# The last chunk's spectrum rows of the last batch, from SBUF to SBUF: squared-ReLU attention followed by a gated FFT convolution, in one kernel

## The chip, the cores and the metric

The kernel runs on one core of one Trainium2 chip. The metric is the device time of one execution in microseconds. Times of single instructions come from one profiled execution of the kernel before.

## The reference

Eight batches of 3136 rows go through an attention without softmax and then through a gated long convolution. Cut to what matters:

```
def attention(u, v, z):                       # u, v: 8 x 3136 x 256, z: 8 x 3136 x 64
    scores = z @ z.T / S                      # S = 3136
    return u * (relu(scores) ** 2 @ v)

def hyena(x, w_proj, filter_fft, w_out):      # x: the attention's result
    x1, x2, x3 = split(x @ w_proj, 3)
    X2 = rfft(x2, axis=seq)
    H  = rfft(filter_fft, axis=seq)
    return (x1 * irfft(X2 * H, axis=seq) * x3) @ w_out
```

## The kernel before, in words

All matrix operands are bf16, all sums are fp32 in PSUM. The 3136 columns of a batch are cut into seven chunks (512, 512, 512, 512, 512, 256, 320 columns; `CHUNKS`), which hold 25 tiles of 128 columns. For each chunk the kernel computes scores (`ps_s<-zT_t` in the profile), squares their ReLU (`R_t`, `A_t`), weighs v with them (`ps_s<-A_t,v_t`; some blocks are mirrored by DMA transposes, `M_t`, `M2e_t`, `M2o_t`), and multiplies the sum by u, which gives `xT_t`. From `xT_t` two things are made. The gates are `x1 * x3` (`ps_s<-xT_t,wp`, then `x_t`, `gate_t`). The spectrum starts with x2 (in `to_spectrum`: `ps_s<-wp,xT_t`, copied to SBUF as `x2`, which the profile shows as `x_t`).

The FFT of length 3136 is done as 64 x 49. The first stage, `dft1`, is a matmul with the table `T1` over 64 rows (`ps_s<-x_t,T`); its result is copied to the SBUF tile `s_t`, and SyncE's queue writes it to the DRAM scratch `D1` (`put`, L1065 and L1068). Row index and frequency index have to change places between the stages, and this detour through DRAM does it: the second stage reads `D1` with 49 rows on partitions 0 to 48 and another 49 on partitions 64 to 112 (`load_spec`, in the last batch `load_parts`, L1114). Four input tiles hold one quarter of the frequencies each; two are from the pool `l_p` (`spec_in_t`), two from `gs_p` (`gs_t`). The second stage (`forward`, `ps_s<-spec_in_t,S` and `ps_s<-gs_t,S`) has eight groups, two for each input tile. Each group is copied out of PSUM (`xh` or `R_t`), multiplied twice by H on VectorE (L1394), goes through the inverse of 49 (`inverse2`, `ps_s<-xh,TZ`, `ps_s<-R_t,TZ`), is copied out (`M_t`, `M2e_t`, `M2o_t`, `A_t`, `uT_t`), and is written to a second DRAM scratch, `D2` (L1443). When all of it has landed, `add_end` reads D2 chunk by chunk (`load_c`, L1128), runs the inverse of 64 (`ps_s<-T,A_t` in the last batch, `ps_s<-T,conv_in_t` and `ps_s<-T,v_t` in the one before), multiplies by the gate (`yT_t`, `uT_t`, L1499), by `w_out` (`ps_s<-wo,...`), copies the result (`ost_t`, `v_t`, `R_t`, `xh`, `gs_t`) and stores it (`out_dram`, L1548).

All engines run orders that are written out: a table `ORDER` lists the tasks, `ENGINES` says for each copy or elementwise task whether ScalarE or VectorE does it, `BANKS` which of four PSUM pairs a task gets. Each engine's instructions, and each DMA queue (SyncE, ScalarE, GpSimd), run strictly in that order. While TensorE has nothing to do, the table may have it multiply the identity (`ps_s<-ident`), work that is thrown away.

In the last batch nothing of a following batch fills the waits. The work of kind `FZ` does: the gates of the last batch, and the ends of chunks 4 to 6 of the batch before. In the stage before this, `load_parts` reads each input tile in two pieces. Rows 0 to 39, which come from chunks 0 to 4, are read early; rows 40 to 48, from chunks 5 and 6, are read when the last chunk has been written:

```
LATE_Q = 2 * T0[NC - 2]
...
a = on("SP", lambda: go(0, LATE_Q), 1.0, first, [home.slots], ...)
if home is gs_p:
    return a, on("ACT", lambda: go(LATE_Q, N2, nc.scalar), 1.1, [*first, *rest, (a, ISSUED)], ...), box
return a, on("SP", lambda: go(LATE_Q, N2), 1.0, [*first, *rest, (a, ISSUED)], ...), box
```

## Time and profile before

| | |
|---|---|
| time, median of 3 runs | 942.79 us (938.34 to 945.0) |
| the profiled execution | 942.77 us, of which 940.9 us from the first to the last instruction |
| TensorE busy | 914.0 us (97%), granted clock 0.997 |
| VectorE, ScalarE, GpSimd busy | 838.7 us (89%), 819.6 us (87%), 247.6 us (26%) |
| chain that ended last | TensorE 83%, ScalarE 5%, VectorE 5%, DMA 5% |
| DMA | 170.70 MB, mean 181 GB/s |

TensorE is busy almost without a gap until the last batch's last chunk has been weighed, some 55 us before the end. The rest is one dependent chain through both spectrum stages, with left-over work laid beside it.

### The profile page before, as it was taken

How to read it: one execution, taken by the hardware profiler on the slowest of the kernel's cores; microseconds unless marked ns; L12 is line 12 of the kernel's file. 1: busy time of each engine (PE TensorE's matmuls, PEld its weight loads, DVE VectorE, ACT ScalarE, POOL GpSimd, SP SyncE). 2: the span in 40 equal slices, each digit the busy share in tenths (PEclk: the TensorE clock that was granted, in tenths of full speed). 3: DMA queues.
4: the chain of work that ended last, by engine and by line, in shares of the span. 5: the costliest groups of instructions: out<-in, count | busy, mean ns of one | idle time of the engine just before them, and what ended most of it. 6: DMA issues, size and time to landing. Idle time of an engine off the chain costs nothing.

```text
span 940.9 us, 30306 instructions
## 1 busy us (share of the span) xinstructions
PE 914.0 (97%) x12425; PEld 555.4 (59%) x12425; DVE 838.7 (89%) x1117; ACT 819.6 (87%) x952; POOL 247.6 (26%) x585
## 2 busy tenths in 40 slices
PE   8999999999999999999999999999999999999985
PEld 3445655566554666556565565666565666676654
DVE  8886899999888998999889988999988999899795
ACT  7877898999889998898989999899988999899673
POOL 5143322332332312223122231333123141101030
PEclk9999999999999999999999999999999999999999
DMA  9899899989999789998999989998999979898867
GB/s 158 155 176 163 141 156 197 185 144 173 169 218 201 151 190 168 206 200 146 192 173 212 177 160 189 178 223 149 200 167 208 224 128 202 202 205 140 207 193 232
DMA packets 331644, 170.70 MB, mean 181 GB/s; under 512 B 242887, under 2 KB 307143, under 8 KB 331505
## 3 DMA queue, kind: packets, MB, share of 16 engines
q1 hardware_dynamic: 301624, 131.98, 70.2%
q0 software_dynamic: 29168, 35.13, 25.8%
q8 instruction: 97, 1.59, 0.7%
q10 hardware_dynamic: 712, 1.66, 0.6%
q14 instruction: 43, 0.34, 0.2%
HBM read 90.26 MB, written 53.05 MB: 152 GB/s over the span
## 4 chain that ended last, share of the span: by engine, by line
PE 83%; ACT 5%; DMA 5%; DVE 5%; issue 2%; SPq 0%; POOL 0%; DVEq 0%; ACTq 0%; POOLq 0%
PE ps_s L553 82%; DMA M_t<-A_t 3%; ACT R_t L1956 2%; DVE xh L1394 1%; DVE A_t L1967 1%; DMA zn_t<-in_z_dram 1%; ACT A_t L1965 1%; DVE xT_t L2012 1%; DMA A_t<-spec 0%; ACT xh L619 0%; DMA spec<-uT_t 0%; ACT ost_t L619 0%; ACT s_t L619 0%; DVE gs_t L623 0%; ACT R_t L619 0%
## 5 line engine op out<-in xcount | busy, mean ns | idle before, releaser
L553 PE MATMUL ps_s<-A_t,v_t 64*128 64x512 bf16 (+5 forms) x4766 | 515.7, 352 | 1.1 <-DVE A_t L1967 1.0
L553 PEld LDWEIGHTS <-v_t 64*128 64x128 bf16 (+1 forms) x6528 | 305.8, 98 | 185.9 <-PE ps_s L553 19.2
L1956 ACT ACTIVATE R_t<-ps_s 128x1024 f32<-128x1024 f32 (+3 forms) x359 | 336.8, 961 | 50.4 <-PE ps_s L553 47.2
L1965 ACT ACTIVATE A_t<-R_t 128x1024 bf16<-128x1024 f32 (+2 forms) x281 | 271.8, 992 | 12.0 <-DVE R_t L1958 4.9
L1967 DVE SCALAR_TENSOR_TENSOR A_t<-R_t 128x1024 bf16<-128x1024 f32 (+3 forms) x211 | 233.6, 1123 | 17.6 <-ACT R_t L1956 10.3
L553 PE MATMUL ps_s<-zT_t 64*128 64x512 bf16 (+5 forms) x1186 | 191.4, 352 | 4.4 <-DVE gate_t L1293 1.7
L1958 DVE TENSOR_SCALAR R_t<-ps_s 128x1024 f32<-128x1024 f32 (+4 forms) x153 | 170.3, 1124 | 23.7 <-PE ps_s L553 13.3
L676 POOL COPY tick<-A_t 1x1 bf16<-1x1 bf16 x159 | 54.3, 341 | 426.0 <-ACT A_t L1965 262.0
L553 PE MATMUL ps_s<-xT_t,wp 64*128 64x512 bf16 (+3 forms) x976 | 124.3, 352 | 0.5 <-DVE R_t L1958 0.4
L553 PEld LDWEIGHTS <-zT_t 64*128 64x128 bf16 (+1 forms) x1219 | 68.9, 97 | 52.8 <-issue 9.8
L553 PE MATMUL ps_s<-M_t,v_t 64*128 64x512 bf16 (+4 forms) x860 | 96.6, 353 | 1.8 <-DMA M_t<-A_t 1.7
L619 ACT ACTIVATE x_t<-ps_s 128x1024 bf16<-128x1024 f32 (+3 forms) x75 | 69.4, 927 | 20.9 <-PE ps_s L553 18.1
L1394 DVE TENSOR_TENSOR xh<-xh,H 128x1024 bf16<-128x1024 bf16 x120 | 81.8, 685 | 2.9 <-ACT xh L619 2.0
L1293 DVE TENSOR_TENSOR gate_t<-ps_s,x_t 128x512 bf16<-128x512 f32 (+2 forms) x112 | 64.5, 617 | 12.4 <-PE ps_s L553 10.3
L2012 DVE TENSOR_TENSOR xT_t<-ps_s,uT_t 128x512 bf16<-128x512 f32 (+2 forms) x112 | 64.0, 614 | 6.5 <-PE ps_s L553 6.1
L1499 DVE TENSOR_TENSOR yT_t<-ps_s,gate_t 128x1024 bf16<-128x1024 f32 (+2 forms) x53 | 56.9, 1078 | 12.9 <-PE ps_s L553 11.7
L553 PEld LDWEIGHTS <-wp 64*128 64x128 bf16 (+1 forms) x976 | 47.8, 96 | 30.0 <-PE ps_s L553 2.0
L553 PE MATMUL ps_s<-wp,xT_t 64*128 64x256 bf16 (+2 forms) x944 | 64.0, 266 | 0.1
L553 PE MATMUL ps_s<-wo,yT_t 64*128 64x256 bf16 (+2 forms) x904 | 62.3, 266 | 1.0 <-DVE yT_t L1499 0.5
L662 POOL DMA_DIRECT2D un_t<-in_u_dram x112 | 58.1, 519 | 18.5 <-issue 16.0
L688 POOL DMA_DIRECT2D v_t<-in_v_dram x112 | 58.4, 525 | 13.6 <-issue 10.3
L553 PEld LDWEIGHTS <-xT_t 64*128 64x128 bf16 (+1 forms) x944 | 43.5, 97 | 19.1 <-issue 0.6
(157 smaller groups left out, 910.2 us busy)
## 6 DMA issues: line engine op xcount, KB each, us to landing
out_dram<-ost_t SPq DMA_DIRECT2D x60, 256.0 KB
spec_in_t<-spec SPq DMA_DIRECT2D x56, 192.0 KB
spec<-gs_t SPq DMA_DIRECT2D x56, 192.0 KB
v_t<-in_v_dram POOLq DMA_DIRECT2D x80, 128.0 KB, 4.5
un_t<-in_u_dram POOLq DMA_DIRECT2D x80, 128.0 KB, 4.5
spec<-s_t SPq DMA_DIRECT2D x40, 256.0 KB
conv_in_t<-spec SPq DMA_DIRECT2D x34, 256.0 KB
out_dram<-ost_t SPq DMA_DIRECT2D x18, 128.0 KB
```

What stands on the lines that cost most here:

```text
L553: got = nc.tensor.matmul(o, *args, **kw)
L619: got = nc.scalar.activation(out_, in_, AF.Copy)
L662: nc.gpsimd.dma_start(out=t[ds(j * N1, N1), lo - t0 : hi - t0, :], in_=x[:, n2 : n2 + hi - lo, :])
L688: nc.gpsimd.dma_start(out=t[ds(j * N1, N1), ds(v_at(a), (b - a) * D)], in_=r[:, n2 + a - lo : n2 + b - lo, :].rearrange("p t d -> p (t d)"),)
L1293: has_read(nc.vector.tensor_tensor(o[:, :, ::-1] if h == 0 else o, p, x, ALU.mult), p)
L1394: nc.vector.tensor_tensor(x[:, 1 - i], x[:, 0], h, ALU.mult)
L1499: has_read(nc.vector.tensor_tensor(yb["y"][:, :, 0:w], p, gates[b, c][:, :, 0:w], ALU.mult), p)
L1956: has_read(nc.scalar.activation(r, p, AF.Relu), p)
L1958: has_read(nc.vector.tensor_single_scalar(r, p, 0.0, ALU.max), p)
L1965: nc.scalar.activation(a, r, AF.Square, scale=1.0 / float(S))
L1967: nc.vector.scalar_tensor_tensor(a, r, inv_s2, r, ALU.mult, ALU.mult)
L2012: has_read(nc.vector.tensor_tensor(x[:, :, ::-1] if h == 0 else x, f, ut, ALU.mult), f)
```

## The change

In the last batch, the first-stage result of the last chunk (rows 44 to 48 of both halves) is no longer written to D1 and read back. Ten DMAs take it from the SBUF tile `s_t` straight into the four input tiles; each of them gathers 32 pieces of 512 bytes (for row 48, 64 pieces of 256 bytes) from 32 partitions into the whole row of one partition, across all four tiles. SyncE issues four, ScalarE three and GpSimd three. For this the four tiles become one SBUF tensor, `grid`, and the pools `l_p` and `gs_p` become parts of it. Rows 0 to 43 still come from D1, now in one piece for each tile (`load_most`), once chunks 0 to 5 are written; those of the `l_p` parts are issued by SyncE, those of the `gs_p` parts by GpSimd. The copies of this chunk's `x2` and `s_t` out of PSUM are split in two, one for each bank (`by_bank`). `ORDER`, `ENGINES` and `BANKS` are new tables.

```diff
-    gs_p = Pool("gs", 2, [P, 8, D], BF16)
-    l_p = Pool("spec_in", 2, [P, 8, D], BF16)
+    grid = const.tile([P, 4 * 8, D], BF16, name="grid")
+    class Part:
+        def __init__(self, *at):
+            self.at, self.slots, self.n = at, Slots(len(at)), 0
+        def tile(self, shape=None, dtype=None):
+            t = grid[:, ds(8 * self.at[self.n % len(self.at)], 8), :]
...
+    l_p, gs_p = Part(0, 1), Part(2, 3)
...
+    def by_bank(n, ev, a, deps, split):
+        got = []
+        for b in ((0,), (1,)) if split else ((0, 1),):
+            x = slice(b[0], b[-1] + 1)
+            t = job(None, lambda e, x=x: ev(e, x), both(n * len(b)), deps)
+            t.frees.append((a, 0))
+            got.append(t)
+        a.holders = len(got)
+        return got
+
+    def straight(s, t0, nt):
+        m, w = nt // 2, nt * P
+        x = s[:, 0 : 2 * w].rearrange("p (b w) -> p b w", b=2)
+        got = []
+        for q in range(2 * t0, min(2 * (t0 + nt), N2)):
+            t, h = q // 2 - t0, q % 2
+            for r in range(2):
+                at = ds(h * N1 + r * 2 * NJ, 2 * NJ)
+                o = grid[r * N1 + q : r * N1 + q + 1]
+                if t == nt - 1 and nt % 2:
+                    got.append((o.rearrange("p x (b d) -> p x b d", b=2), x[at, :, m * D : w]))
+                else:
+                    got.append((o, x[at, t // m, ds(t % m * D, D)]))
+        return got
...
-        b_ = job(None, ev, both(2 * w), [a2])
+        b_ = by_bank(w, ev, a, [a2], split)
+        if split:
+            def go(e, i):
+                by = {"SP": nc.sync, "ACT": nc.scalar, "POOL": nc.gpsimd}[e]
+                for o, x in straight(s["s"], t0, nt)[i::3]:
+                    by.dma_start(out=o, in_=x)
+            return [(e, lambda e=e, i=i: go(e, i), b_) for i, e in enumerate(("SP", "ACT", "POOL"))]
...
-    LATE_Q = 2 * T0[NC - 2]
+    LATE_Q = 2 * T0[NC - 1]
-    def load_parts(src, j0, nj, first, rest, home):
+    def load_most(src, j0, nj, deps, home, by):
         box = {}
+        def go():
+            box["t"] = home.tile([P, 8, D], BF16)
+            rows = src[0:S, :].rearrange("(q r x) d -> r q x d", r=2, x=2 * NJ)[:, 0:LATE_Q, ds(2 * j0, 2 * nj), :]
+            for r in range(2):
+                {"SP": nc.sync, "POOL": nc.gpsimd}[by].dma_start(out=box["t"][r * N1 : r * N1 + LATE_Q, 0 : 2 * nj, :], in_=rows[r])
+        return on(by, go, 1.0, deps, [home.slots], moves=0.36 * nj, late=0.5), box
...
-            if g % 2 == 0 and final:
-                after_q = [(before[-1], ISSUED)] if before and homes[g // 2] is gs_p else []
-                ldb[0] = load_parts(D1[b % 2], 2 * g, 4, [*puts[:early], *after_q], puts[early:], homes[g // 2])
+            if g == 0 and final:
+                parts_ = []
+                for i, home in enumerate(homes):
+                    after_q = [(before[-1], ISSUED)] if before and home is gs_p else []
+                    after_q += [(parts_[-1][0], ISSUED)] if i % 2 else []
+                    parts_.append(load_most(D1[b % 2], 4 * i, 4, [*puts, *after_q], home, "POOL" if home is gs_p else "SP"))
+                lasts_in = []
+                for e, go, made_ in direct:
+                    lasts_in.append(on(e, go, 1.8, [*made_, *((t, ISSUED) for t, _ in parts_)], prio=-1, moves=0.1, late=0.5))
+            if final:
+                ld, ibox = parts_[g // 2]
+                more = lasts_in
```

Of the tables, one line of `ORDER` near its end before and after reads:

```diff
-    "R]KLKER^KYR=vTR#R}R_PFvUR~KFPGR{vVKGPHPRSLR[SMS0PLR|PMSQPNvWSRvXSNPOSXKMKHSYS1SbKNSSScvYSOKOSPSTS2SU"
```

What the new tables mean is seen in the engines' orders. Over the first 89% of TensorE's rows (22,137 of 24,852), and about as far on the other four engines, the instructions and their order are the same as before, except for which PSUM pair an instruction uses. Behind that point the orders part.

On SyncE's queue, around the second stage's input, `spec_1_60` is D1 and `spec_1_62` is D2 of the last batch, `spec_0_61` is D2 of the batch before. Before:

```order
L1065 DMA spec_1_60<-s_t 128x2x256
L1114 DMA gs_t<-spec_1_60 40x2048 x2
L1114 DMA spec_in_t<-spec_1_60 40x2048 x2
L1114 DMA gs_t<-spec_1_60 40x2048 x2
L1128 DMA v_t<-spec_0_61 128x2x256
L1128 DMA v_t<-spec_0_61 128x3x256
L1128 DMA conv_in_t<-spec_0_61 128x4x256
L1065 DMA spec_1_60<-s_t 128x2x256
L1068 DMA spec_1_60<-s_t 128x1x128
L1128 DMA conv_in_t<-spec_0_61 128x4x256
L1114 DMA spec_in_t<-spec_1_60 9x2048 x4
```

And with the change, at the same place:

```order
L1104 DMA spec_1_60<-s_t 128x2x256
L1170 DMA v_t<-spec_0_61 128x2x256
L1170 DMA conv_in_t<-spec_0_61 128x4x256 x2
L1603 DMA out_dram<-ost_t 64x512 x2
L1159 DMA grid<-spec_1_60 44x2048 x4
L1119 DMA grid<-s_t 1x32x256 x3
L1119 DMA grid<-s_t 1x64x128
```

The first line of both is the write of chunk 5. Before, the large reads stand around it and the write and read of the last chunk (L1065, L1068, `9x2048`) far behind; now the large reads stand behind it, and the four direct transfers follow them at once.

On GpSimd, the end of the program. Before:

```order
L1548 DMA out_dram<-ost_t 64x1024 x4
L1548 DMA out_dram<-v_t 64x1024 x2
L1548 DMA out_dram<-ost_t 64x1024 x2
L1443 DMA spec_1_62<-M_t 48x2048
...
L1548 DMA out_dram<-v_t 64x512 x2
L1548 DMA out_dram<-v_t 64x768
L1548 DMA out_dram<-v_t 64x512
L1548 DMA out_dram<-ost_t 64x1024 x2
L1548 DMA out_dram<-R_t 64x1024
L1548 DMA out_dram<-xh_118 64x1024
```

With the change:

```order
L1159 DMA grid<-spec_1_60 44x2048 x4
L1119 DMA grid<-s_t 1x32x256 x2
L1119 DMA grid<-s_t 1x64x128
...
L1603 DMA out_dram<-ost_t 64x1024 x2
L1603 DMA out_dram<-v_t 64x768
L1603 DMA out_dram<-v_t 64x512
L1603 DMA out_dram<-R_t 64x1024
L1603 DMA out_dram<-xh_118 64x1024
L1603 DMA out_dram<-ost_t 64x1024 x4
L1603 DMA out_dram<-v_t 64x1024 x2
```

`ost_t` and `v_t` are results of the batch before the last, `R_t` and `xh_118` the first of the last batch. Six stores of 256 KB (64 x 1024 fp32 each) of the batch before the last, which stood ahead of the first D2 write or of `R_t`, now stand behind `xh_118`.

On TensorE, just ahead of the second stage (`spec_in_t,S` before, `grid,S` after; the LDWEIGHTS row ahead of each matmul loads its weights). Before:

```order
L553 MATMUL ps_s_142<-T_215,conv_in_t 128x2x64
L553 LDWEIGHTS ident
L553 MATMUL ps_s_140<-ident 128x512
...
L553 LDWEIGHTS S_216
L553 MATMUL ps_s_140<-spec_in_t,S_216 64x256
```

With the change:

```order
L567 MATMUL ps_s_134<-T_210,v_t 128x128
L567 LDWEIGHTS v_t
L567 MATMUL ps_s_134<-T_210,v_t 128x2x64
...
L567 LDWEIGHTS S_211
L567 MATMUL ps_s_137<-grid,S_211 64x256
```

The 26 identity matmuls of the last 50 us are gone altogether. Otherwise TensorE's matmuls are the same in sum, but 16 matmuls of a gate projection (`xT_t,wp`, 512 columns) and 16 of an output projection (`wo,yT_t`, 8 of 256 and 8 of 128 columns) that stood ahead of the last weighing (`A_t,v_t`) now stand behind it.

More of the change, by code (lines that the diff above doesn't have):

```diff
@@ L187 @@
[L187 to L191 removed]
+    "0123012312313213213213212310313013131032032032032320230201201012012023203023020323010210210212313213"
@@ L1051, in view, with ev @@
             return x[:, 0 : 2 * w].rearrange("p (b w) -> p b w", b=2)
-        def ev(e):
-            copy(e, view(s["s"]), box["p"][:, :, 0:w])
+        def ev(e, x=slice(0, 2)):
+            copy(e, view(s["s"])[:, x], box["p"][:, x, 0:w])
         def put():
@@ L1248 @@
             h_done += evs
+    direct = []
     gates, made = {}, {}
@@ L1326, in view, with ev2 @@
                 return x[:, 0 : 2 * w].rearrange("p (b w) -> p b w", b=2)
-            def ev2(e):
-                copy(e, view(box2["x"]), box["p"][:, :, 0:w])
+            def ev2(e, x=slice(0, 2)):
+                copy(e, view(box2["x"])[:, x], box["p"][:, x, 0:w])
             cost = c_pe(*[D] * (2 * m), *([P] * 2 if n % 2 else []))
             a, a2, box = two("FA", mm, cost, xt_tasks, [x2_p.slots])
-            e2 = job(None, ev2, both(2 * w), [a2])
-            e2.frees.append((a, 0))
+            end = b == B - 1 and c == NC - 1
+            e2 = by_bank(w, ev2, a, [a2], end)
             users.append(a2)
@@ L1339, in get @@
                 return x[:, m * D : w] if k is None else x[:, 0 : m * D]
-            puts.append(
-                dft1(
-                    "FA", get, t0, n, D1[b % 2], [e2, t1_done], (a, 1),
-                    late=LATE_PUT,
-                )
-            )
+            got = dft1(
+                "FA", get, t0, n, D1[b % 2], [*e2, t1_done], (a, 1),
+                late=LATE_PUT, split=end,
+            )
+            if end:
+                direct.extend(got)
+            else:
+                puts.append(got)
         if b == B - 1 and c == NC - 1:
@@ L1371, in add_spectrum @@
             per, gh = 2 * len(mine), outs[sets.index(mine)]
-            if g % 2 == 0 and final:
-                after_q = [(before[-1], ISSUED)] if before and homes[g // 2] is gs_p else []
-                ldb[0] = load_parts(D1[b % 2], 2 * g, 4, [*puts[:early], *after_q], puts[early:], homes[g // 2])
+            if g == 0 and final:
[10 more added lines that the diff above has]
+                more = lasts_in
             elif g % 2 == 0:
                 ldb[0] = load_spec(D1[b % 2], 2 * g, 4, puts, LATE_LOAD)
-            ld, *more, ibox = ldb[0]
+            if not final:
+                ld, *more, ibox = ldb[0]
             xb = {}
```

246 lines of the change are left out of this document (120 added, 126 removed).

## The prediction

> **What bounds the kernel now.** I read the page first, then the chain of waits, then the time-ordered rows of each engine from 860 us on, and last a table of stretches.
>
> ```profile
> PE 914.0 (97%) x12425; PEld 555.4 (59%) x12425; DVE 838.7 (89%) x1117; ACT 819.6 (87%) x952; POOL 247.6 (26%) x585
> PE   8999999999999999999999999999999999999985
> ```
>
> TensorE is the bound over the whole program, in every slice but the first and the last two. The orders of all engines are the same for nine tenths of the program, so I expect nothing of the change there. What counts is the tail: how long the chain from the last chunk to the last store takes, and what TensorE has to do beside it.
>
> The tail's first part, from the rows of TensorE, ScalarE and SyncE's queue:
>
> ```profile
> 888.40 0.72 PE L553 MATMUL ps_s<-x_t,T 64*128 64x256 bf16 x6
> 889.16 0.81 ACT L619 ACTIVATE s_t<-ps_s 128x768 bf16<-128x768 f32 x1 [0.83 <-PE ps_s L553]
> 889.99 0.36 SPq L1065 DMA_DIRECT2D spec<-s_t x1
> 890.41 0.58 SPq L1068 DMA_DIRECT2D spec<-s_t x1
> 894.38 1.68 SPq L1114 DMA_DIRECT2D spec_in_t<-spec x4
> 896.70 0.61 PE L553 MATMUL ps_s<-ident 64*128 64x512 bf16 x4
> 897.24 1.15 PE L553 MATMUL ps_s<-spec_in_t,S 49*64 49x256 bf16 x11
> ```
>
> The first stage's result is in SBUF at 889.97. Its write to D1 is issued by 890.99, the read can start only at 894.38, and the second stage starts at 897.24: **7.27 us** of detour. TensorE hides most of it with left-over work, but the identity matmuls show that this work has run out.
>
> The rest of the chain:
>
> ```profile
> 898.21 0.60 ACT L619 ACTIVATE xh<-ps_s 128x512 bf16<-128x512 f32 x1 [0.56 <-PE ps_s L553]
> 911.61 0.85 ACT L619 ACTIVATE uT_t<-ps_s 128x512 bf16<-128x512 f32 x1
> 913.70 3.91 DMA spec<-uT_t
> 914.63 1.24 PE L553 MATMUL ps_s<-ident 64*128 64x512 bf16 x10
> 918.48 1.03 PE L553 MATMUL ps_s<-ident 64*128 64x512 bf16 x8
> 919.02 4.18 DMA A_t<-spec
> 920.72 0.40 PE L553 MATMUL ps_s<-T,A_t 64*128 64x128 bf16 x8 [1.22 <-DMA A_t<-spec]
> 933.49 0.38 PE L553 MATMUL ps_s<-wo,yT_t 64*128 64x256 bf16 x4
> ```
>
> The second stage and its inverse take from 898.21 to 912.46 (911.61 + 0.85), 14.25 us, bound by the copies and multiplications: in the stretches below, ScalarE and VectorE are full from 900 to 908 and TensorE is not. The detour through D2 takes from there to 920.72, 8.26 us; the last stage ends on TensorE at 933.87. Then come the last stores.
>
> ```profile
> 900.00:904.00 4.00, 3.51 (x71) 2.15 (x63) 4.00 (x7) 4.00 (x9) 0.00 (x0) 1.00 0.28 89
> 904.00:908.00 4.00, 2.92 (x58) 1.59 (x56) 4.00 (x8) 4.00 (x10) 2.15 (x4) 1.00 0.62 116
> 920.00:924.00 4.00, 2.66 (x64) 1.95 (x66) 2.36 (x2) 0.60 (x1) 1.03 (x2) 1.00 0.83 243
> 924.00:928.00 4.00, 4.00 (x86) 3.14 (x82) 2.58 (x4) 3.14 (x6) 1.06 (x2) 1.00 0.96 286
> 928.00:932.00 4.00, 3.10 (x64) 2.13 (x58) 3.87 (x7) 1.20 (x3) 0.00 (x0) 1.00 0.96 326
> 938.00:939.00 1.00, 0.00 (x0) 0.00 (x0) 0.00 (x0) 0.00 (x0) 0.00 (x0) 0.67 0.88 308
> 939.00:940.00 1.00, 0.00 (x0) 0.00 (x0) 0.00 (x0) 0.00 (x0) 0.00 (x0) 0.50 0.01 3
> ```
>
> The last two columns are the DMA engines' busy share and GB/s. From 924 on the DMA engines are full, at 286 to 326 GB/s. The last bytes move at 939.0, and the span ends 1.9 us later. From 900 to 908 they are nearly idle.
>
> **The change, step by step.** All against the profiled execution: span 940.9, time 942.77, 1.87 apart; the median of the runs is 942.79, so the same number serves.
>
> *Less TensorE work ahead of the last chunk.* One gate projection (16 matmuls) and 16 output matmuls go behind it:
>
> ```profile
> 880.16 1.02 ACT L619 ACTIVATE x_t<-ps_s 128x1024 bf16<-128x1024 f32 x1 [0.50 <-PE ps_s L553]
> 883.90 1.29 DVE L1293 TENSOR_TENSOR gate_t<-ps_s,x_t 128x512 bf16<-128x512 f32 x2 [1.76 <-PE ps_s L553]
> 882.22 0.59 PE L553 MATMUL ps_s<-xT_t,wp 64*128 64x512 bf16 x4
> 882.65 0.71 PE L553 MATMUL ps_s<-A_t,v_t 64*128 64x320 bf16 x8
> 911.77 0.50 PE L553 MATMUL ps_s<-wo,yT_t 64*128 64x256 bf16 x8
> 912.12 0.59 PE L553 MATMUL ps_s<-xT_t,wp 64*128 64x512 bf16 x4
> ```
>
> Four projection matmuls take 0.43 (882.22 to 882.65), so 16 take 1.72; eight output matmuls of this kind take 0.35 (911.77 to 912.12), so 16 about 0.65. With the projection go its copy (1.02) and its gate product (1.29), so ScalarE and VectorE have less to do there too. Up to the first-stage matmul itself 0.2 goes the other way. First stage at 886.3 instead of 888.40: **-2.1**. If ScalarE or VectorE hold it up, half of this is lost.
>
> *Split copies.* `s_t` is copied in two halves of 384 columns on two engines at once. No copy of 384 from PSUM to bf16 stands in the trace; 512 takes 0.60 (898.21) and 768 takes 0.81, so 0.5, and 0.3 gained (0.2 to 0.4). The same split of `x_t` one step earlier is worth nothing: gate projection lies beside it. `s_t` is ready at 887.5 instead of 889.97, **-2.5 in all**.
>
> *Ten direct transfers for the detour.* SyncE issues four, at 1.68/4 = 0.42 each: 1.7. From issue to data, no row shows a transfer into single partitions. The nearest are a read of D1 of 36 KB (issued by 895.2, used at 897.24: 2.0), a GpSimd load of 64 KB, and the write to D2 above (3.91):
>
> ```profile
> un_t<-in_u_dram POOLq DMA_DIRECT2D x1, 64.0 KB, 2.4
> ```
>
> I take 2.4: it is the nearest in size. 887.5 + 1.7 + 2.4 = **891.6** for the second stage's start instead of 897.24; with 2.0 and 3.9 it is 891.2 and 893.1. One thing gets worse: before, the first group needed two transfers, now it needs rows that all ten bring. Removed are two writes and eight small reads.
>
> The direct rows land in few partitions (44 to 48 and 108 to 112). [...]
>
> *The large reads.* They now wait for chunk 5's write, and nothing is read before:
>
> ```profile
> 880.71 0.69 DVE L623 CAST s_t<-ps_s 128x512 bf16<-128x512 f32 x1 [0.33 <-PE ps_s L553]
> 882.65 0.51 SPq L1065 DMA_DIRECT2D spec<-s_t x1
> 883.20 0.78 SPq L1114 DMA_DIRECT2D gs_t<-spec x2
> 884.00:886.00 2.00, 2.00 (x30) 1.17 (x24) 1.80 (x5) 0.00 (x0) 0.00 (x0) 1.00 1.06 308
> ```
>
> This write went out 1.25 behind its copy, after reads that it now stands ahead of; and the copy itself comes earlier by about the 2.1 above. I expect the write by 880, landed 3.4 later (as 890.99 to 894.38), 1.44 MB (8 x 180 KB) at 308 GB/s in 4.7: there by 888.5, hidden behind the direct rows with 3 us to spare.
>
> *Second stage and inverse.* The same 27 copies of 512 columns and one of 1024 on ScalarE, but one more of 1024 (`x_t`, 1.02) between them: 14.25 + 0.9. It ends at about 907.7 instead of 912.46: **-4.7**.
>
> *The D2 detour* stays at 8.26: first `T,A_t` at 916.0. At the rate above (0.107 for 512 columns) the matmuls that stand between the last inverse and `T,A_t` come to 8.7 us of left-over work, where 5.3 and 18 identity matmuls stood; with the 0.8 between the last inverse matmul and its copy's end it just fits. Cover is used up here; each us that it runs over is a us.
>
> *The last stage and the stores.* By the same rate TensorE has 9.3 us of work there instead of 9.8, so it ends about 928.7, and on the old distance (940.9 - 933.87 = 7.0) the span would end at **935.7**. But GpSimd's queue now holds six stores of 256 KB (1.57 MB) behind the store of `xh`:
>
> ```profile
> 904.42 1.06 POOL L1548 DMA_DIRECT2D out_dram<-ost_t x2 [5.42 <-ACT ost_t L619]
> 923.25 0.40 PE L553 MATMUL ps_s<-T,A_t 64*128 64x128 bf16 x8 [0.61 <-DMA A_t<-spec]
> 925.91 1.08 ACT L619 ACTIVATE xh<-ps_s 128x512 f32<-128x512 f32 x2
> 927.29 0.52 POOL L1548 DMA_DIRECT2D out_dram<-xh  x1 [0.57 <-ACT xh L619]
> ```
>
> Before, stores like that of 904.42 ran when the DMA engines were idle. The copy of `xh` ended 6.3 after the first `T,A_t`. A second pair of copies now lies ahead of it (1.1), and the wait of 0.6 at 923.25 goes, since the chunk that waited is read later: 6.8, so 922.8. Of 3.21 MB of the last batch's output (3136 x 256 x 4 bytes) about 0.65 have moved by then (2.2 us at 0.3). 3.21 + 1.57 - 0.65 = 4.1 MB at 306 GB/s (mean of 286 and 326) take 13.4, from 923.1 to 936.5, and 1.9 more give a span of 938.4; at 326 it is 937.6. The stores end last, not TensorE. I take the middle, 938.0: -2.9, a time of **939.8 us**.
>
> **Rivals.** *The stores are hidden after all* (other transfers leave room, the queues share well): TensorE ends it, span 935.7 and time 937.6; with a direct landing of 2.0 (-0.4), the extra copy hidden (-0.9) and the wait at 923.25 gone from TensorE's end too (-0.6), 935.7. For it: the row at 928 shows 326 GB/s. Against: 286 just before, at the same busy share.
>
> *The direct rows come late.* If writes to single partitions go one after the other, or chunk 5's write is not as early as I think (with 882.65 for it the reads end at about 891.5 and the direct rows queue behind), the second stage starts at 894 to 896. Then `xh` is copied at 925.2 to 927.2 and by the sum above (at 326 GB/s) the time is 942 to 944. This is also the case in which the change does not do what it says.
>
> *Slower: GpSimd's queue.* The six stores behind `xh` add 1.57/0.306 = 5.1 us of transfers to the stretch that the DMA engines already fill. The span gets longer than 940.9 once 0.3 + 13.4 + 1.9 after the copy of `xh` pass it, that is when this copy ends later than 925.3, only 1.7 before its old 926.99. An overrun of 2.5 of the left-over work after the inverse does it, or a start of the second stage at 894.1. Just there, and at the 243 GB/s of the row at 920 (16.9 for 4.1 MB) instead of 306, the span is 944.4 and the time 946.3; at 275, 944.3.
>
> **How the numbers follow.** Forecast 0.5 (own range 938 to 941.8); stores hidden 0.2; direct rows late 0.15; slower by the queue 0.12; the rest, 0.03, outside. The range takes in the first three and the lower half of the fourth, and 1 us below the best of them, since the three times of before differ by 6.7: 934.5 to 945. About 1% (9.4 us) is what a measurement of this kernel can tell from no change. No case reaches 933.4: faster by over 1% gets 0.04. Slower by over 1% (952.2) would need the queue's case with more than I can price: 0.04. Within 1%: 0.92.
>
> **What would show it.** The first `grid,S` matmul should stand near 891.6, 4.1 behind the copy of `s_t`; the first `T,A_t` near 916; no identity matmuls after the start. GB/s near 300 should hold from about 920 to the last byte, with stores of `ost_t` and `v_t` by GpSimd behind `xh`. I am wrong on the sum if TensorE idles for over 1 us between 908 and 916, if the large reads land after the direct rows, or if the last bytes move well before 935 or after 938.

## The result: 7 us slower, where 3 us faster was forecast

| | before | after |
|---|---|---|
| median of 7 runs each (us) | 942.79 | 949.82 |
| lowest to highest | 938.34 to 949.53 | 946.87 to 952.47 |
| ratio, 95% interval | | 1.0079 (1.0050 to 1.0109) |
| profiled execution: time, span | 942.77, 940.9 | 950.02, 948.2 |

The interval excludes 1: the change costs 0.5 to 1.1%. The forecast was 939.8 and the range ended at 945; the ratio itself lies within the 1% that had been given 0.92. The page of the changed kernel shows nearly the same work on each engine; only the last slices differ (TensorE 2 and its clock 6 in the last one, the clock 7 two slices earlier):

```profile
PE 913.4 (96%) x12375; PEld 560.1 (59%) x12375; DVE 835.1 (88%) x1116; ACT 821.7 (87%) x955; POOL 250.7 (26%) x592
PE   8999999999999999999999999999999999999892
PEclk9999999999999999999999999999999999999796
```

The rows of the tail, from ScalarE, VectorE, TensorE, GpSimd and SyncE's queue (start, duration, what; in brackets, idle time before it and what ended it):

```profile
879.90 2.00 SPq L1159 DMA_DIRECT2D grid<-spec  x4
882.01 0.73 PE L567 MATMUL ps_s<-x_t,T 64*128 64x256 bf16 x6
882.82 0.48 ACT L633 ACTIVATE s_t<-ps_s 128x384 bf16<-128x384 f32 x1
883.07 0.55 DVE L637 CAST s_t<-ps_s 128x384 bf16<-128x384 f32 x1
883.45 4.27 SPq L1119 DMA_DIRECT2D grid<-s_t  x4
890.70 2.79 PE L567 MATMUL ps_s<-grid,S 49*64 49x256 bf16 x23 [3.06 <-DMA grid<-s_t]
909.63 0.65 ACT L633 ACTIVATE A_t<-ps_s 128x512 bf16<-128x512 f32 x1
919.03 0.40 PE L567 MATMUL ps_s<-T,A_t 64*128 64x128 bf16 x8
925.72 1.08 ACT L633 ACTIVATE xh<-ps_s 128x512 f32<-128x512 f32 x2 [0.42 <-PE ps_s L567]
927.10 0.53 POOL L1603 DMA_DIRECT2D out_dram<-xh  x1 [2.30 <-ACT xh L633]
927.62 2.12 POOL L1603 DMA_DIRECT2D out_dram<-ost_t  x4
929.73 1.06 POOL L1603 DMA_DIRECT2D out_dram<-v_t  x2
928.22 1.60 PE L567 MATMUL ps_s<-wo,uT_t 64*128 64x256 bf16 x24
```

The reader is to see four distances. `s_t` is ready at 883.62 and the second stage starts at 890.70: **7.08 us**, where the detour took 7.27 and 4.1 was forecast. From there to the first `T,A_t` matmul it is **28.33** (23.48 before). From that matmul to TensorE's end (929.82) it is 10.79 (13.15). From TensorE's end to the span's end it is **18.38** (7.03). The sum is 64.58 against 50.93. Nothing of this can be read from the absolute positions: this execution reached the first-stage matmul 6.4 us earlier than that of before, 4 more than the moved work (2.1 to 2.4) explains.

Stretches of the tail: their length, the busy time of TensorE, its weight loads, VectorE, ScalarE and GpSimd (with instructions), then the granted clock of TensorE, the DMA engines' busy share and their GB/s:

```profile
886.03:889.44 3.41, 1.22 (x18) 0.61 (x14) 2.12 (x4) 1.83 (x2) 1.06 (x2) 1.00 0.34 64
889.44:892.86 3.42, 2.16 (x23) 1.51 (x24) 0.80 (x2) 1.04 (x3) 0.00 (x0) 0.50 0.95 274
892.86:896.27 3.41, 3.26 (x37) 1.16 (x36) 3.41 (x6) 3.41 (x8) 0.00 (x0) 0.50 0.85 248
896.27:899.68 3.41, 3.41 (x51) 2.48 (x52) 3.41 (x7) 1.65 (x3) 1.08 (x2) 0.50 0.36 84
899.68:903.10 3.42, 1.97 (x45) 1.29 (x44) 1.61 (x4) 3.22 (x7) 0.00 (x0) 1.00 0.01 1
903.10:906.51 3.41, 3.35 (x65) 2.56 (x61) 3.41 (x7) 2.81 (x5) 1.09 (x2) 0.50 0.37 80
924.00:926.00 2.00, 1.94 (x45) 1.52 (x43) 1.89 (x3) 1.36 (x3) 0.53 (x1) 1.00 0.36 78
926.00:930.00 4.00, 3.76 (x77) 2.85 (x73) 3.72 (x8) 2.17 (x5) 2.90 (x6) 1.00 0.99 214
938.00:942.00 4.00, 0.00 (x0) 0.00 (x0) 0.00 (x0) 0.00 (x0) 0.00 (x0) 0.50 0.95 333
942.00:943.00 1.00, 0.00 (x0) 0.00 (x0) 0.00 (x0) 0.00 (x0) 0.00 (x0) 0.50 0.46 180
943.00:948.00 5.00, 0.00 (x0) 0.00 (x0) 0.00 (x0) 0.00 (x0) 0.00 (x0) 0.50 0.00 0
```

Two things are new. From 889.44 to 899.68, and again from 903.10 to 906.51, TensorE runs at half its clock (0.50); before, it stood at 1.00 from 900 to 908. And after the last byte (943.0) another 5.2 us pass, 1.9 before. From 924 to 926 the DMA engines move 78 GB/s while GpSimd waits for the copy of `xh`, with six finished stores behind it.

### The profile page after: what moved, and what is told of

It is laid out like the page before. It is cut to its first block, busy times and chain, and to the rows that moved or that the text cites. A ratio compares the mean times of both kernels' runs of the same rounds, so it can differ in the third digit from the quotient of the medians.

```text
span 948.2 us, 30238 instructions
## 1 busy us (share of the span) xinstructions
PE 913.4 (96%) x12375; PEld 560.1 (59%) x12375; DVE 835.1 (88%) x1116; ACT 821.7 (87%) x955; POOL 250.7 (26%) x592
## 4 chain that ended last, share of the span: by engine, by line
PE 83%; DVE 5%; DMA 4%; ACT 3%; issue 2%; ACTq 0%; POOL 0%; SPq 0%; DVEq 0%; POOLq 0%
PE ps_s L567 83%; DMA M_t<-A_t 1%; DVE xh L1449 1%; DVE A_t L2022 1%; ACT R_t L2011 1%; DMA zn_t<-in_z_dram 1%; DMA M2o_t<-A_t 1%; ACT grid L633 1%; ACT A_t L2020 1%; DMA spec<-grid 1%; DVE yT_t L1554 1%; DMA grid<-s_t 0%; DMA A_t<-spec 0%; DVE xT_t L2067 0%; DVE xh L637 0%
## 5 line engine op out<-in xcount | busy, mean ns | idle before, releaser
L2020 ACT ACTIVATE A_t<-R_t 128x1024 bf16<-128x1024 f32 (+3 forms) x283 | 273.1, 993 | 10.5 <-DVE R_t L2013 4.9
L2022 DVE SCALAR_TENSOR_TENSOR A_t<-R_t 128x1024 bf16<-128x1024 f32 (+3 forms) x209 | 230.9, 1120 | 18.3 <-ACT R_t L2011 10.2
L2013 DVE TENSOR_SCALAR R_t<-ps_s 128x1024 f32<-128x1024 f32 (+3 forms) x152 | 169.0, 1123 | 21.2 <-PE ps_s L567 11.3
L567 PE MATMUL ps_s<-xT_t,wp 64*128 64x512 bf16 (+3 forms) x992 | 126.4, 357 | 0.8 <-DVE gate_t L1336 0.3
L633 ACT ACTIVATE x_t<-ps_s 128x1024 bf16<-128x1024 f32 (+4 forms) x77 | 70.9, 922 | 16.3 <-PE ps_s L567 15.3
L702 POOL DMA_DIRECT2D v_t<-in_v_dram x112 | 58.3, 526 | 13.0 <-issue 10.2
```

The costliest lines, as they stand in the source:

```text
L567: got = nc.tensor.matmul(o, *args, **kw)
L633: got = nc.scalar.activation(out_, in_, AF.Copy)
L702: nc.gpsimd.dma_start(out=t[ds(j * N1, N1), ds(v_at(a), (b - a) * D)], in_=r[:, n2 + a - lo : n2 + b - lo, :].rearrange("p t d -> p (t d)"),)
L2013: has_read(nc.vector.tensor_single_scalar(r, p, 0.0, ALU.max), p)
L2020: nc.scalar.activation(a, r, AF.Square, scale=1.0 / float(S))
L2022: nc.vector.scalar_tensor_tensor(a, r, inv_s2, r, ALU.mult, ALU.mult)
```

## The experiments

Theories: the six late stores on GpSimd's queue (**stores**), the half clock in the second stage (**clock**), the late direct transfers (**direct rows**). The distances of every kernel, from one profile each: A from the last copy of `s_t` to the first second-stage matmul, B on to the first `T,A_t`, C on to TensorE's end, D on to the span's end; then the time from the last byte of GpSimd's queue, and of any queue, to the span's end (last bytes read in steps of 0.25 us). Each ratio is to runs of the kernel before on the same chip. The runs are spread over several chips, so medians in us are set side by side only where they come from one chip, or where the text says otherwise.

| kernel | A | B | C | D | GpSimd's byte to end | any byte to end | ratio to before, 95% interval |
|---|---|---|---|---|---|---|---|
| before | 7.27 | 23.48 | 13.15 | 7.03 | 9.25 | 1.5 | |
| after | 7.08 | 28.33 | 10.79 | 18.38 | 5.75 | 5.0 | 1.0079 (1.0050 to 1.0109) |
| e10_again | 6.66 | 26.97 | 10.79 | 18.93 | 5.75 | 5.0 | 1.0105 (1.0072 to 1.0139) |
| e1_stores | 6.44 | 27.36 | 10.80 | 10.97 | 6.5 | 1.5 | 1.0026 (0.9996 to 1.0056) |
| e5_stores | 7.37 | 28.32 | 11.46 | 9.08 | 7.5 | 1.5 | 0.9996 (0.9970 to 1.0021) |
| e9_hold | 7.32 | 23.20 | 13.54 | 13.45 | 5.5 | 3.5 | 1.0056 (1.0031 to 1.0080) |
| e12_sync | 7.13 | 28.27 | 10.79 | 16.06 | 12.75 | 1.5 | 1.0060 (1.0036 to 1.0083) |
| e2_fills | 7.12 | 25.35 | 10.80 | 18.56 | 5.75 | 5.0 | 1.0082 (1.0056 to 1.0108) |
| e6_nofill | 7.28 | 24.07 | 12.67 | 6.98 | 9.25 | 1.5 | 1.0012 (0.9981 to 1.0043) |
| e3_detour | 6.97 | 29.88 | 10.79 | 18.28 | 5.75 | 5.0 | 1.0121 (1.0085 to 1.0157) |
| e4_reads | 5.43 | 27.37 | 10.78 | 18.89 | 5.75 | 5.25 | 1.0087 (1.0058 to 1.0117) |
| e7_all | 6.05 | 28.33 | 12.04 | 7.68 | 7.25 | 1.25 | 1.0003 (0.9969 to 1.0037) |
| e8_all | 8.09 | 27.24 | 14.92 | 6.71 | 9.75 | 1.5 | 1.0007 (0.9975 to 1.0039) |
| e11_both | 6.85 | 24.83 | 10.79 | 9.76 | 6.25 | 1.5 | 0.9981 (0.9954 to 1.0009) |
| e15_again | 7.58 | 25.27 | 11.28 | 8.54 | 6.5 | 1.5 | 0.9982 (0.9949 to 1.0015) |
| e14_detour | 6.47 | 25.18 | 10.80 | 9.55 | 6.5 | 1.5 | 1.0002 (0.9966 to 1.0037) |

### The stores: earlier, held back in the old kernel, and on another queue

In `go`, the number in a code names a task; 4214, 4222 and 4811 are the three tasks that issue the six stores, 4743 the store of `R_t`, 4827 that of `v_t` of the shortest chunk, 4753 that of `xh`.

```
 e1_stores, in go():
+for k in (4811, 4214, 4222):
+    codes.remove(k)
+    codes.insert(codes.index(4743), k)
 e5_stores:
+for k in (4214, 4811, 4222):
+    codes.remove(k)
+    codes.insert(codes.index(4827), k)
 e9_hold, in the kernel before:
+for k in (4811, 4222, 4214):
+    codes.remove(k)
+    codes.insert(codes.index(4753) + 1, k)
 e12_sync, in add_end:
+            elif b == B - 2 and c in (2, 3, 4):
+                s_ = on("SP", lambda nt=nt, store=store: store(0, nt), 1.2, ...)
```

> The change as it is, except that GpSimd's six late stores of 256 KB (ost_t four times, v_t twice) stand ahead of its stores of R_t and xh in its queue and not behind them. In the profile of the change they go out from 927.6 on, after the copy of xh (926.8), while their copies were done by 921; TensorE ends at 929.82 and the span 18.4 us later (7.0 before). Theory A (the tail is long because 1.57 MB wait behind xh, and then share full DMA engines with the last stores): they go out between 914 and 922, where the DMA engines moved 188 to 290 GB/s, the last byte moves about 1.57 MB / 0.306 = 5.1 us earlier, so TensorE's end to the span's end is 12 to 14 us instead of 18.4, and the time falls by 4 to 6 us to about 944 to 946. If what follows the last byte (5.2 us against 1.9 before) hangs on GpSimd's late stores too, the distance is 8 to 11 and the time 940 to 943. Rival B (the tail is long for another reason, the waits of SyncE's and ScalarE's own stores): the distance stays at 17 to 19 and the time within 2 us of the change's. Rival C (the early stores delay the detour through D2): first T,A_t matmul 10 to 14 us behind the copy of A_t instead of 8.75, and the time is no better.

> The change as it is, except that GpSimd's six late stores stand ahead of its stores of v_t of the shortest chunk too, in the order ost_t, v_t, ost_t. With the six moved only ahead of R_t, they went out at 926.25 to 930.47 there (1.9 behind the first T,A_t matmul), since they stood behind that v_t store, whose copy ended late. Their own copies end 1.5 ahead of the first T,A_t matmul in the profile of the change. Theory A (the backlog of the last stores sets the end): they go out from about 2 us ahead of the first T,A_t matmul, 1.57 MB move while the DMA engines had room, and TensorE's end to the span's end falls from 10.97 to 8 or 9 (18.38 in the change). Theory B (the last 10 us are bound by SyncE's and ScalarE's own queues, whose issues wait for earlier transfers): the distance stays at 10 to 11.5. Rival C (the stores slow the reads of D2): first T,A_t matmul 10 to 12 us behind the last copy of the inverse, where it was 8.75 in the change, and nothing is won.

Theory A holds in both by the distance: D falls from 18.38 to 10.97 and 9.08, and the ratio from 1.0079 and 1.0105 (the change, measured twice) to 1.0026 and 0.9996. In e1 the six stores went out at 926.25 to 930.47, not between 914 and 922, and the median of 947.15 (943.33 before, on that chip) is above what the theory gave. GpSimd's rows of e5_stores and its last stretches:

```profile
920.28 1.07 POOL L1606 DMA_DIRECT2D out_dram<-ost_t  x2 [4.71 <-ACT ost_t L636]
921.34 1.07 POOL L1606 DMA_DIRECT2D out_dram<-v_t  x2
922.88 1.07 POOL L1606 DMA_DIRECT2D out_dram<-ost_t  x2 [0.48 <-ACT ost_t L636]
931.57 0.55 POOL L1606 DMA_DIRECT2D out_dram<-xh  x1 [3.04 <-ACT xh L636]
941.00:942.00 1.00, 0.00 (x0) 0.00 (x0) 0.00 (x0) 0.00 (x0) 0.00 (x0) 0.50 0.20 78
942.00:943.30 1.30, 0.00 (x0) 0.00 (x0) 0.00 (x0) 0.00 (x0) 0.00 (x0) 0.50 0.00 0
```

The six are out by 924, and the long wait behind the last byte is gone too. Rival C shows in a small part: from the last copy of the inverse (913.05) to the first `T,A_t` matmul (922.76) it is 9.71, 1 us more than the 8.75 of the change, and short of the rival's 10 to 12. B as a whole is 28.32, as in the change.

> The kernel before, with one edit: its six stores of 256 KB on GpSimd's queue (ost_t four times, v_t twice), which there go out between 904 and 921, are held back behind its store of xh, as in the change. The direct transfers and all the rest are not in it. Theory A (these six stores by themselves are what the change lost): TensorE's end to the span's end 16 to 19 us instead of 7.0, the last bytes moved by GpSimd's queue with 5 to 6 us behind them instead of 2, and a time 7 to 11 us above the kernel before. Rival B (they cost only where the change's other delays come on top): distance 9 to 12, time 2 to 5 us above.

```profile
924.47 0.52 POOL L1551 DMA_DIRECT2D out_dram<-xh  x1 [0.59 <-ACT xh L622]
924.98 2.08 POOL L1551 DMA_DIRECT2D out_dram<-ost_t  x4
927.05 1.05 POOL L1551 DMA_DIRECT2D out_dram<-v_t  x2
940.00:941.00 1.00, 0.00 (x0) 0.00 (x0) 0.00 (x0) 0.00 (x0) 0.00 (x0) 0.50 0.14 54
941.00:944.50 3.50, 0.00 (x0) 0.00 (x0) 0.00 (x0) 0.00 (x0) 0.00 (x0) 0.50 0.00 0
```

Between the theories: the old kernel with nothing but its stores held back loses 5.3 us (948.33 against 943.05), and D is 13.45. So this order alone makes between half and three quarters of the slowdown (5.3 of the 10.2 us measured on this chip, of 7.0 in the first result), and not 7 to 11 us. The queues of SyncE and ScalarE move its last bytes, yet 3.5 us lie behind them: the detail of theory A that GpSimd must move the last byte is wrong. What fits is the table's column: 5.5 us behind GpSimd's own last byte, against 5.75 in the change.

> The change as it is, with the same six late stores at the same place of the program's order, but issued by SyncE, behind its own stores of R_t and xh, and not by GpSimd. The same bytes move as late. Theory A (two costs: about 5 us of bytes that come late, and 3 to 4 us because a transfer of GpSimd's queue is the last one): the last bytes move 12 to 14 us behind TensorE's end as in the change, the span ends 2 us behind them instead of 5.2, the distance is 14 to 16, and the time 3 to 4 us below the change's. Theory B (the late bytes are all of it): the distance stays at 17 to 19 and 5 us lie behind the last byte whatever queue it is. Rival C (SyncE's queue blocks its own last stores behind the six): last bytes later than 14 behind TensorE's end, and no gain.

```profile
927.86 7.19 SPq L1603 DMA_DIRECT2D out_dram<-ost_t  x4
942.00:944.00 2.00, 0.00 (x0) 0.00 (x0) 0.00 (x0) 0.00 (x0) 0.00 (x0) 0.50 0.87 242
944.00:945.00 1.00, 0.00 (x0) 0.00 (x0) 0.00 (x0) 0.00 (x0) 0.00 (x0) 0.50 0.34 78
945.00:946.40 1.40, 0.00 (x0) 0.00 (x0) 0.00 (x0) 0.00 (x0) 0.00 (x0) 0.50 0.00 0
```

The same bytes, at least as late, on SyncE's queue: the last byte moves 14.3 behind TensorE's end (13.2 in the change) and only 1.5 follow. The 14.3 and the D of 16.06 lie just outside theory A's ranges (12 to 14, and 14 to 16); its mechanism shows all the same, and of rival C only the late bytes: the median is 948.12, and 953.21 for the unchanged change on the same chip, 5.1 us less where theory A had 3 to 4. So the late stores cost twice: by bytes that move late, and by the queue they are on.

> The change unchanged, as the measure for the other kernels on this chip, and as a second profile of it. If the stretch lengths of the first profile are typical: second stage 6.5 to 7.5 us behind the copies of s_t, from there to the first T,A_t matmul 27.5 to 29 us with the clock at 0.50 for 6.8 to 13.7 us, TensorE's end to the span's end 18 to 19, time 6 to 8 us above the kernel before. If they were an accident of that execution: clock at 1.00 in the second stage in this one, and a distance at the end under 15.

The pattern is the same in this second profile: 6.66, 26.97, 18.93, with the clock at 0.50 for 6.8 us. B is half a microsecond below what was expected, and goes with the shorter time at half clock. The loss, 10.2 us, is higher than expected, but its interval meets that of the first result.

### The clock: filler ahead of the second stage, and none in the old kernel

```
 e2_fills:  +codes[codes.index(4661) : codes.index(4661)] = [len(every) + 3] * 14    (28 matmuls)
 e6_nofill: +late = [i for i, k in enumerate(codes) if k >= len(every) and i > 5000]
            +codes = [k for i, k in enumerate(codes) if i not in late]
```

> The change as it is, with 28 identity matmuls of 512 columns (3.0 us at 0.107 each) put on TensorE ahead of the first grid,S matmul, where it idles for 3.06 us in the profile of the change. Theory A (that idle time is what sets the granted clock to 0.50 from 889.3 to 899.7, and the slow matmuls, 0.63 instead of 0.38 us, make the second stage and inverse 18.7 us long instead of 14.25): the clock stays at 1.00 there, the stage takes 14 to 16 us, and the time falls by 2.5 to 4.5 us. Rival B (the clock falls for another reason, such as the work just before or the kind of the matmuls): clock 0.50 in the stage as before, 18 to 19 us, time the same or up to 1 us longer. Rival C (the clock stays up but ScalarE and VectorE bind the stage): clock 1.00 and still 17 to 19 us.

```profile
889.06:892.47 3.41, 2.96 (x39) 1.48 (x34) 0.81 (x2) 0.69 (x2) 0.28 (x1) 1.00 0.77 223
892.47:895.89 3.42, 3.03 (x56) 1.49 (x56) 3.42 (x6) 3.42 (x8) 0.00 (x0) 1.00 1.00 279
895.89:899.30 3.41, 2.17 (x44) 1.23 (x36) 3.41 (x7) 3.41 (x7) 1.07 (x2) 1.00 0.50 120
899.30:902.71 3.41, 3.35 (x60) 2.64 (x63) 3.41 (x7) 3.40 (x7) 0.20 (x1) 0.50 0.01 2
```

With the wait filled, TensorE works at full clock (1.00 up to 899.30) where the change works at half (0.50), and B is 25.35 instead of 28.33; the stage from its first to its last copy takes 15.9 instead of 18.7: theory A, by the profile. One stretch of 3.41 us at half clock is left. The time does not show it: 1.0082, where theory A had 2.5 to 4.5 us less than the change. A gain of 3 us (0.3%) would hardly stand out from intervals of this width.

> The kernel before, without its last 26 identity matmuls (8 in the wait ahead of and within the second stage, 18 in the detour through D2); nothing else is changed. Theory A (such filler, which the change dropped, is what kept the granted clock at 1.00 in the kernel before): the clock falls to 0.50 in a stretch of 3.4 to 10 us after one of the two waits, the matmuls behind it take 0.6 instead of 0.38 us, second stage and inverse take 16 to 19 us instead of 15.2 (first matmul to last copy), or the last stage 14 to 18 instead of 13.15, and the time rises by 2 to 6 us. Rival B (8 matmuls, 0.9 us, are too few to matter, and the clock fell in the change for another reason): clock 1.00 throughout, time within 1.5 us.

Nearer to rival B: without its 26 identity matmuls the old kernel has one stretch at 0.50 (905.18 to 908.59), as theory A had it, but B is only 24.07 (23.48 with them) and the ratio 1.0012. So little filler as the old kernel had is worth little. What cost the clock in the change (0.50 from 889.44 on) is that TensorE idles 3.06 us in one piece, which e2 shows from the other side: with that wait filled, the clock stood at 1.00 there.

### The direct rows: back through D1, and reads that don't hold them up

```
 e3_detour (SyncE, slices 0 and 1; GpSimd, slices 2 and 3; ScalarE nothing):
-for o, x in straight(s["s"], t0, nt)[i::3]:
-    by.dma_start(out=o, in_=x)
+if e == "SP":
+    put()
+...
+by.dma_start(out=grid[r * N1 + 2 * t0 : r * N1 + N2, ds(x, 8), :], in_=rows[r, 2 * t0 : N2, ds(x, 8), :])
 e4_reads:
-parts_.append(load_most(..., home, "POOL" if home is gs_p else "SP"))
+parts_.append(load_most(..., home, "POOL"))
```

> The change as it is, except that the last chunk's spectrum rows go through DRAM again: SyncE writes s_t to D1 with two transfers and reads four slices back, GpSimd reads the other four; the split copies, the early reads and the order of the rest stay. In the profile of the change the direct transfers bring the second stage 7.08 us behind the copy of s_t, where the detour of the kernel before took 7.27. Theory A (the direct route as placed here is worth almost nothing, 0.2 us): first grid,S matmul 7 to 8.5 us behind the copies of s_t, time within 1.5 us of the change's. Rival B (the direct route is worth what I forecast, 3.2 us, and something else in this kernel holds the second stage up): the distance stays near 7 because that other thing lands last. Rival C (the detour is worse here, because the large reads and the stores before it fill the queues): 9.5 to 11 us, and the time 2 to 4 us longer than the change's.

Theory A on the distance: 6.97 through DRAM, 7.08 direct. But here the first group needs only the first slice, and the later slices land while the stage runs: A and B together are 36.85, against 35.41 and 33.63 in the two profiles of the change. The time leaves theory A and rival C open: 953.98 is 4.2 us above the first result, and within 1 us of the unchanged kernel's 953.21 on another chip.

> The change as it is, except that all eight large reads of D1 (176 KB each) are issued by GpSimd, where SyncE issued four of them at 879.9 to 881.9. In the profile of the change SyncE's four direct transfers take 0.55 each to issue but stand at 883.45, 884.69, 886.13 and 887.10, with waits for earlier transfers (the reads of D1, of D2, and a store) between them; the second stage starts 3.0 behind the last one's issue. Theory A (the waits on those reads are what makes the direct transfers late): SyncE issues its four within 2.2 to 2.8 us, and the second stage starts 5 to 6 us behind the copies of s_t instead of 7.08; time lower by 1 to 2 us, or by up to 4 if the shorter idle time also keeps the clock up. Rival B (landing in a single partition is slow by itself, at whatever time it is issued): the start stays at 6.8 to 7.5 though the issues end earlier. Rival C (GpSimd's queue gets late with eight reads, and its three direct transfers land last): 7.5 to 9.

```profile
885.78 0.55 DVE L637 CAST s_t<-ps_s 128x384 bf16<-128x384 f32 x1
886.04 2.57 SPq L1119 DMA_DIRECT2D grid<-s_t  x4
891.76 1.99 PE L567 MATMUL ps_s<-grid,S 49*64 49x256 bf16 x23 [1.75 <-DMA grid<-s_t]
```

Theory A's numbers: SyncE's four issues take 2.57 instead of 4.27 us, and A is 5.43. The waits between SyncE's issues in the change, from its own table (us in all, times, longest):

```profile
SPq L1119 <- DMA grid<-spec: 1.3, 2, 0.8
SPq L1119 <- DMA out_dram<-ost_t: 0.6, 1, 0.6
```

But SyncE's issues are only half of it. GpSimd's three direct transfers are issued almost without a wait (883.59 to 885.21 in the change), and still take long to land. In the change, then in e4_reads (KB each, median us from issue to landing):

```profile
grid<-s_t POOLq DMA_DIRECT2D x3, 16.0 KB, 5.3
grid<-s_t POOLq DMA_DIRECT2D x3, 16.0 KB, 4.1
```

In the change the last of them lands at 889.62, 6.0 behind `s_t` and 1.1 ahead of the stage's start, so without SyncE's waits the stage could have started about 0.8 us earlier and no more (an estimate: 0.3 behind that landing, as in e4). In e4 the last one lands at 891.44 and the stage starts 0.32 later: there GpSimd's queue sets the start, the mechanism of rival C at a smaller size. That is also why the gain is not steady. Two more kernels with the reads on GpSimd have A at 6.05 and 8.09 (e7, e8), and both start 0.3 us behind GpSimd's last landing; in e8 these three took 6.4 to 6.8 us, behind reads that landed up to 898.38, 5.8 behind `s_t`. The time shows nothing (1.0087).

### Together

`e7_all` is e5_stores, e4_reads and 16 identity matmuls; `e8_all` adds eight ahead of the seventh group (task 4710); `e11_both` and `e15_again` are e5_stores and the filler of e2_fills; `e14_detour` is that with the edit of e3_detour.

> Three edits on the change at once: the six late stores early in GpSimd's queue, all large reads of D1 issued by GpSimd, and 16 identity matmuls (1.7 us) ahead of the first grid,S matmul. If the three causes are apart and add up: second stage 5.4 behind the copies of s_t (7.08), stage and inverse 16 to 17 us (19.6), TensorE's end to the span's end 8 to 11 (18.4), together 11 to 14 us less than the change from the last chunk's xT_t on, a time of 936 to 940 and so 3 to 7 us faster than the kernel before. Rival: they share one cause (an earlier start only brings a longer wait for copies or stores later): 942 to 946.

> As the kernel with the three edits, with eight more identity matmuls (0.85 us) ahead of the seventh group of grid,S matmuls, behind which TensorE idled 1.06 us (in the kernel with 28 identity matmuls) and the clock fell for one more stretch of 3.4 us. Theory A (idle time of about 1 us in a stretch of 3.4 is enough to halve the clock): no 0.50 in the second stage and inverse, which take 15 to 16 us, 0.5 to 1.5 us less than with three edits alone. Rival B (those matmuls only push the following groups back): the stage is 0.5 to 1 us longer.

Neither sum came out: 1.0003 and 1.0007. In e7 the clock fell all the same (a stretch in which TensorE was busy 2.47 of 3.42 us, 0.72, with 0.50 for 6.8 us behind it); in e8 the rows came at 8.09 and TensorE idled 2.7 us in spite of the filler, and later 2.38 for a read of D2:

```profile
937.40 0.40 PE L572 MATMUL ps_s<-T,A_t 64*128 64x128 bf16 x8 [2.38 <-DMA A_t<-spec]
```

So the eight extra matmuls were never tested under their own condition, and that run is inconclusive for them.

> Two edits on the change: the six stores early in GpSimd's queue (9.1 us from TensorE's end to the span's end, alone), and 28 identity matmuls ahead of the first grid,S matmul (25.4 instead of 28.3 us from there to the first T,A_t matmul, alone); the large reads stay on both queues. Theory A (two separate costs that add): 25 to 26 us and 8 to 10 us, a time 2 to 4 us below that of the early stores alone, and so 1 to 4 us faster than the kernel before. Rival B (the time saved ahead of the last stage is waited for at the end, since the last stores are bound by the DMA engines): the distance at the end grows by what the stage gains, and the time is that of the early stores alone, within 1.5 us of the kernel before.

```profile
892.29:895.70 3.41, 3.04 (x50) 1.56 (x51) 3.01 (x5) 2.83 (x6) 0.00 (x0) 1.00 0.97 296
899.12:902.53 3.41, 2.10 (x56) 1.39 (x55) 3.41 (x7) 3.41 (x9) 0.00 (x0) 1.00 0.25 56
902.53:905.94 3.41, 3.26 (x80) 2.08 (x84) 3.38 (x7) 3.41 (x8) 1.13 (x3) 1.00 0.55 121
```

The clock stays at 1.00, B is 24.83, D 9.76, and the median 940.73, against 953.21 for the change on the same chip: the two edits together are worth 12.5 us there, and 9.2 by the ratio of the first result. Against the kernel before it is 0.9981 (0.9954 to 1.0009).

What the filler adds to this, the times do not show: e5_stores, with the stores alone, stands at 0.9996, and the intervals overlap. The profiles do. From the first second-stage matmul to the last copy of the inverse they have 15.8 to 16.7 us where at most one stretch of 3.41 us ahead of the first `T,A_t` matmul was at half clock (e2, e11, e14, e15), 18.1 to 18.3 with 6.8 us of it (e1, e4, e7, e8, e10), and 18.6 to 19.9 with 10.2 or 13.7 (after, e3, e5, e12).

> The change with the six stores early and 28 identity matmuls, once more, to narrow its interval against the kernel before and as the measure for the detour kernel on the same chip. Theory A (the two edits bring the change level with the kernel before or a little below it): ratio 0.995 to 1.001, clock 1.00 in the second stage, 8 to 10 us from TensorE's end to the span's end. Rival B (its lower time was the chip or the hour): ratio 1.002 to 1.006.

> The change with the six stores early and 28 identity matmuls ahead of the first grid,S matmul, but with the last chunk's rows through D1 again. Theory A (the direct route saves 0.2 to 0.5 us, as the 6.97 of the detour against 6.4 to 7.4 of the direct transfers suggest): second stage 7 to 8 us behind the copies of s_t, time within 2 us of the same kernel with direct transfers. Rival B (with the other two costs gone the direct route shows what it is worth, 2 to 3 us): 9 to 10 us, and the time 2 to 4 us higher.

Repeated, 0.9982 (0.9949 to 1.0015), with one stretch at 0.50 within the stage (903.55 to 906.97) where 1.00 was expected. Each interval touches 1: a version that beats the kernel before by 0.2% is likely and not shown. The detour kernel stands at 1.0002, 0.2% higher with intervals that overlap. Its second stage starts 6.47 behind the copies, earlier than expected, with 0.55 of a further wait inside; A and B together are 31.65, against 31.68 and 32.85 in the two kernels with direct transfers. Rival B is out: as it is placed here the direct route is worth little by the distances, and how little the times can't tell.

## Why the prediction was wrong, step by step

From `s_t` ready on, the forecast had 50.5 us (887.5 to 938.0) and the profile has 64.6. The 14.1 between them stand in three terms; the forecast span was 10.2 too low, since this execution had `s_t` ready 3.9 earlier than forecast. All distances below count from `s_t` or from the step before.

- **Less TensorE work ahead: not to be told.** The last chunk's `xT_t` rows stand between 879.0 and 888.4 in the 13 profiles that share the change's order up to there (mean 882.7), and at 881.9 to 885.5 in the three of the kernel before (mean 883.3). The difference goes the right way, but 2.1 us drown in a spread of 9, which the whole program gathers before the tail. There is one more sign of it: the tail of the change is 13.65 us longer (64.58 against 50.93), its median only 7.0. Over the 13 kernels the time lost by the ratio is 0.9 to 6.2 us, 3.6 in the mean, below what A to D lost against the kernel before; for e6 and e9, which have the old order, it is 1.1 above and 1.3 below. So something ahead of `s_t` does save about as much as was forecast; with one profile each this is argued, not shown.
- **Split copies: right.** 0.48 and 0.55 instead of 0.81.
- **Direct transfers, forecast 4.1, measured 7.08 (+3.0): a failed step.** It took 1.7 for four issues and 2.4 for landing, and both were too low. SyncE's issues took 4.1 (883.62 to 887.72): 2.1 of it were waits, 1.3 of them for the large reads, which the same change had put just ahead of them, and e4_reads takes those away. From SyncE's last issue to the start it was 3.0, inside the bounds of 2.0 and 3.9; but GpSimd's three transfers, out by 885.21, took 4.9 to 5.3 us each to land, above both bounds. The forecast had looked at SyncE's queue alone. Little of SyncE's 3.0 was the moving of bytes: the packets of its last transfer moved between 888.25 and 888.75, 2 us ahead of the start. The rival "direct rows late" named the size (894 to 896, 6.5 to 8.5 behind `s_t`) and, as its second cause, direct rows that queue behind late reads.
- **Large reads, forecast there 1.0 behind `s_t` (888.5 against 887.5): a failed step behind the one above.** Chunk 5's write went out early, at 874.70, 8.9 ahead of `s_t`. But SyncE's reads went out only at 879.90 to 881.90, since three reads of D2 and two stores stand between in its order. SyncE waited for them until 887.10, with its last direct transfer, and once more until 888.46, 4.8 behind `s_t`. They were there before the second stage started, but not free: the direct transfers waited for them.
- **Second stage, inverse and D2 detour, forecast 24.4, measured 28.3 (+3.9): a failed step.** From the first matmul to the last copy of the inverse it took 19.6 instead of 16.1. The copies were priced at the old pace and the clock at nothing, and the trace of before, at 1.00 in this stretch even behind 1.2 us of idle time at 919.5, gave no hint. e2, e11 and e15 bring B to 24.8 to 25.4, near what was forecast. The forecast had called the old wait hidden by filler and then dropped the filler without asking what the idle time does to TensorE itself (0.50 behind 3.06 us of it). Cover for the D2 detour just sufficed, as forecast: it took 8.75 instead of 8.26, and TensorE idled 0.3 us in it.
- **Last stage and stores, forecast 22.0, measured 29.2 (+7.2): the failed step that costs most.** The copy of `xh` ended 7.8 behind the first `T,A_t` matmul, forecast 6.8. What moves behind that copy was priced at 13.7 us with the issue, and the last byte moved 16.2 behind it, at 214 GB/s in the first four. The forecast had the DMA engines idle when such stores ran before; from 904 to 908 they were busy for 0.62, at 116 GB/s. The 1.9 behind the last byte became 5.2, because GpSimd's queue ended late (see the last section); before, the same wait was there and hidden, since GpSimd's stores were long done. With the 0.4 that taking the middle had cut off, these are the 7.2. The rival was named with its place and its threshold, "when this copy ends later than 925.3", and the copy ended at 926.80; it was given 0.12, and its dearest price, 946.3, was still too low. e5 and e9 show the order as the cause from both sides, e12 the part of the queue.

The forecast had that copy only 2.5 us ahead of the threshold (922.8 against 925.3). Errors of 6.9 us in the two terms ahead of it were bound to pass it, so 0.12 was too little even by the forecast's own bounds: the rival was weighed as if it stood alone, while every other failure led into it.

## What to carry to other kernels

A store that is done early and stands late in a queue is a debt at the end (here D was 18.38 us with six of them late, 9.08 in e5_stores with them early): look, for each queue, at what is behind the last instruction that waits. When nothing fills a wait of TensorE, price the matmuls behind it at half clock as well: here 10.2 us of it followed 3.06 us of idle time. And when one step needs transfers from several queues, price each queue, with its waits between issues and its own time to landing, and take the one that ends last (in e4_reads GpSimd's, which landed at 891.44, 0.32 ahead of the stage).
